# Attention and a two-layer network in one kernel: bank pairs declared as single tiles, one visit moved, some transfers queued later

## The chip, the cores and the metric

The kernel runs on one core of one Trainium2 chip. The metric is the device time of one execution in microseconds. The kernel before took 787.15 us, the median of three runs (785.26, 787.15 and 787.8).

## The reference

The input is q, k and v of shape 8 x 8 x 576 x 64 (batch, heads, sequence, head size) in float32. Each sequence is cut into chunks of 64 tokens, and a chunk attends only to itself. The result, with the heads side by side, is x, of 4608 tokens by 512, and goes through two matrix products with a leaky rectifier between them:

```python
scores = 1/sqrt(64) * q_c @ k_c.T            # per batch, head and chunk of 64 tokens
attn   = exp(scores - max(scores)); attn /= sum(attn) + 1e-9
x      = (attn @ v_c), heads side by side     # 4608 x 512
h      = x @ w_in                             # 512 -> 2048
g      = maximum(h, 0) + alpha * minimum(h, 0)
out    = g @ w_out                            # 2048 -> 512
```

## The kernel before

**Tiling.** The 4608 tokens are nine blocks of 512. The first three go through the network directly (lines L454 and L490 of the profile). The other six form three pairs, and a pair goes through both layers by a fast 2 x 2 block scheme with seven products in place of eight. Operands are split into a high and a low part, so each product is three passes. Attention works on blocks of 128 tokens; the attention for a pair is done beside the matmuls of the pair before it.

**A pair.** The first layer of a pair is eight steps (j = 0 to 7, `first_product`). A step holds seven sets of six matmuls on TensorE (`part`, line L764), in the order 5, 7, 1, 6, 3, 4, 2. They go into four PSUM banks: c takes sets 5 and 3, d takes 7 and 4, a takes 1 and 2, e takes 6. Between them ScalarE and VectorE read the banks: ScalarE copies c (L780) and a (L792), VectorE adds d and e to the copies (L781, L797, L798), then forms c+u and d+u (L807), and the rectifier is one ScalarE and one VectorE operation each (L439, L442). The names are: t is "gh", u is "g", h is "gl". After the eight steps the second layer follows (`second_product`, L895), seven products of 48 matmuls each, about 10.56 us each in the profile.

**Banks.** PSUM has eight banks here: two single tiles of the pool `ps_h` (taken anew at each use, two in turn), one tile of two banks `ps_a`, and two tiles of two banks, `ps_pa` and `ps_pb`. The last two pools open when the direct part's four accumulator banks (`ps_oa`, `ps_ob`) have been stored (L524). In a step, a and e are the halves of one `ps_pa` tile and change roles with the parity of j. In the first two pairs c and d are two `ps_h` tiles. In the last pair, where no attention is left, c and d are the halves of one `ps_pb` tile (`fronts`). The framework puts a wait where an instruction touches a tile that another engine still uses.

**Visits.** In the first two pairs, in steps 0, 2, 4 and 6, a joined visit (`joint_visit`) comes first on TensorE: the value products of up to two attention blocks (L420) and the score products of the next two (L289), into `ps_a` and `ps_pb`. The softmax of the new blocks (L301 to L308) and the transposition of 32 x 32 squares (L348, tile `t3`) follow inside the steps on VectorE and ScalarE. The last part of the transposition is done by eight DMAs of 32 KB, `pT<-t3` (L363, `move_blocks`); a value product needs them. There are two `pT` buffers. When both are taken, a block's moves wait in a list, and the next value products send them off at once. The q and k loads (L246, 256 KB each) of the next two blocks and the v loads (L250) go the same way, on SyncE's queue, in the order of issue. Weights stream on GpSimd's queue (L702), 512 KB at a time.

**Order.** A scheduler sets each engine's order. TensorE keeps the program's order; `high_priority` and `issue_after` steer the others.

Of the kernel before, what the change touches and what calls it, by code (L numbers as in the profile page):

```python
# [10 lines left out]
F32 = mybir.dt.float32  # L11
# [59 lines left out]
def tile_local_attention_prelu_ffn(  # L71
# [12 lines left out]
    nc = tc.nc  # L84
    P = 128
    NSUB, C = qT.shape[1], 64
# [8 lines left out]
    TB = 512  # L95
# [146 lines left out]
    def attn_load(s, parts="qkv"):  # L242
        if "q" in parts:
            q_sb, kb = (load.tile([P, H, C], F32, name=name, bufs=2) for name in ("q_sb", "k_sb"))
            for t, src in ((q_sb, qT), (kb, kT)):
                nc.sync.dma_start(out=t, in_=src[:, s].rearrange("p (h t) -> p h t", t=C))  # L246
            qkv[s] = [q_sb, kb, None]
        if "v" in parts:
            v_sb = load.tile([P, DM], F32, name="v_sb", bufs=2)
            loads.append(nc.sync.dma_start(out=v_sb, in_=v[:, s]))  # L250
            qkv[s][2] = v_sb
# [192 lines left out]
    def prelu(g, h, f):  # L444
        negative(g, h)
        rectify(g, h, f)
# [307 lines left out]
    def narrow():  # L754
        return [ps_h.tile([P, TB], F32, name="ps_h") for _ in range(2)]

    def product(ps, w, xs, first):

        passes = [(0, 0), (0, 1), (1, 0)]
        n = len(xs) * 3  # L760
        for m, (l, xl) in enumerate(passes):
            for k, xx in enumerate(xs):
                at = m * len(xs) + k
                pe(nc.tensor.matmul(  # L764
                    woven(ps), lhsT=w[:, l, k * P:(k + 1) * P], rhs=woven(xx[:, xl]),
                    start=first and at == 0, stop=at == n - 1, skip_group_check=not first,
                ))

    def first_product(ops, g, j, visited, fronts, ends, value):

        def part(ps, i, first):
            product(ps, weight("wi", i, j), [ops[i, k] for k in range(2)], first)

        c, d = fronts or narrow()
        a, e = ends[j % 2], ends[1 - j % 2]
        part(c, 5, True)
        part(d, 7, True)
        with tc.high_priority(offset=HIGH):
            t = gp.tile([P, TB], F32, name="gh")
            copied = nc.scalar.copy(t, c)  # L780
            nc.vector.tensor_tensor(t, d, t, op=ALU.add)  # L781
        if visited:
            with tc.high_priority(offset=HIGH), tc.issue_after(copied.ins):
                visit_softmax(*visited)
        part(a, 1, True)
        part(e, 6, True)
        if value is not None:
            with tc.high_priority(offset=HIGH):
                joint_values((value,))
        with tc.high_priority(offset=HIGH):  # L790
            u = gp.tile([P, TB], F32, name="g")
            copied = nc.scalar.copy(u, a)  # L792
        if visited:
            with tc.high_priority(offset=HIGH), tc.issue_after(copied.ins):
                visit_results(*visited)
        with tc.high_priority(offset=HIGH):
            nc.vector.tensor_tensor(u, e, u, op=ALU.add)  # L797
            nc.vector.tensor_tensor(t, t, u, op=ALU.add)  # L798
        for n, f in enumerate((j, JF + j)):
            g[f] = place(rooms[2 * j + n], [P, 2, TB], F32)  # L800
        with tc.high_priority(offset=HIGH):
            prelu(g[JF + j][:, 1], t, JF + j)
        for ps, i, f, col in ((c, 3, j, 1), (d, 4, JF + j, 0)):
            part(ps, i, False)
            with tc.high_priority(offset=HIGH):
                h = gp.tile([P, TB], F32, name="gl")
                nc.vector.tensor_tensor(h, ps, u, op=ALU.add)  # L807
                prelu(g[f][:, col], h, f)
        part(a, 2, False)
        with tc.high_priority(offset=HIGH):  # L810
            prelu(g[j][:, 0], a, j)

    CONVERT = (16, 17, 18, 20, 21, 23, 48, 49, 50, 51, 52, 53, 54, 55)
    AHEAD = 2
# [36 lines left out]
    def second_product(g, b, operands, conversion, end):  # L851
        y = [xp.tile([P, NK, TB], F32, name=name) for name in ("xh", "xl")]
        y11, y12, y21, y22 = y[0][:, :2], y[1][:, :2], y[0][:, 2:], y[1][:, 2:]

        def add(ys, ps):
            for m in range(2):
                nc.vector.tensor_tensor(ys[:, m], ps[m], ys[:, m], op=ALU.add)

        def finish(ys, ps):

            first = (b - PLAIN) * TB
            for m, queue in enumerate((nc.sync, nc.scalar)):
                nc.scalar.copy(ys[:, m], ps[m])
                queue.dma_start(out=outT[(2 + m) * P:(3 + m) * P, first:first + TB], in_=ys[:, m])

        def copy(ys, ps):
            for m in range(2):
                nc.scalar.copy(ys[:, m], ps[m])

        def done(ys, m, half, col):  # L870
            rows = slice((2 * half + m) * P, (2 * half + m + 1) * P)
            cols = slice((b - PLAIN + col) * TB, (b - PLAIN + col + 1) * TB)
            nc.sync.dma_start(out=outT[rows, cols], in_=ys[:, m])


        kept, third = narrow(), wide("ps_pb")
        for i in ORDERS["wo"]:
            if i == 2:
                ps = wide("ps_pa")
            else:  # L880
                ps = third if i in (5, 3) else kept
            for j in range(JF):
                at = JF * ORDERS["wo"].index(i) + j
                if at + AHEAD + EARLIER < 7 * JF:
                    difference(g, at + AHEAD + EARLIER)

                ahead = at + AHEAD + (at < 2)
                if at != 2 and ahead < 7 * JF:
                    with tc.high_priority(offset=2 * HIGH) if at < 2 else nullcontext():
                        operands.append(operand(g, ahead))  # L890
                hi, lo = operands.pop(0)
                w = weight("wo", i, j)
                for m in range(2):
                    for n, (l, xx) in enumerate(((0, hi), (0, lo), (1, hi))):
                        pe(nc.tensor.matmul(  # L895
                            woven(ps[m]), lhsT=w[:, l, m * P:(m + 1) * P], rhs=woven(xx),
                            start=i in (1, 5, 2) and j == 0 and n == 0, stop=j == JF - 1 and n == 2,
                            skip_group_check=i in (6, 7, 3, 4),
                        ))
                if conversion and at in CONVERT:  # L900
                    with tc.issue_after(behind[1][0].ins), tc.issue_after(behind[1][1].ins):
                        conversion.pop(0)()
            if i == 1:
                copy(y11, ps)
            elif i == 5:
                copy(y22, ps)
            elif i == 6:
                copy(y12, ps)
            elif i == 4 and end:
                finish(y21, ps)  # L910
            else:
                ys, half, col = {2: (y11, 0, 0), 7: (y22, 1, 1), 3: (y12, 0, 1), 4: (y21, 1, 0)}[i]
                (copy if i == 4 else add)(ys, ps)
                for m in range(2):
                    done(ys, m, half, col)
# [158 lines left out]
    def joint_values(olds):  # L1074
# [3 lines left out]
        outs = {}  # L1078
        for old in sorted((old for old in olds if old is not None), reverse=True):
            outs[old] = attn_values(old, 0, olds.index(old))  # L1080
        while moves and len(pdiag) < 2:
            move_blocks()
        for s in list(qkv):
            if qkv[s][2] is None and sum(e[2] is not None for e in qkv.values()) < 2:
                attn_load(s, "v")
        if len(olds) == 1:
            ended.append((olds[0], outs[olds[0]]))
        return outs

    VALUES = {0: (-2, -1), 2: (0, None), 4: (2, 1), 6: (4, 3)}  # L1090

    def joint_visit(base, j):
# [5 lines left out]
        for new in range(base + j + 2, base + j + 4):  # L1098
            if new < NSUB:
                attn_load(new, "q")  # L1100
        return [(old, outs.get(old), new, scores.get(new)) for old, new in zip(olds, news)]

    ended = []
    for pair in range(NPAIR):
# [5 lines left out]
        g = {}  # L1110
        joint = []
        for j in range(JF):
            if more and j in VALUES:
                with tc.high_priority(offset=HIGH):
                    joint = joint_visit(base, j)
            if j == 0:
                ends = wide("ps_pa")
                fronts = () if more else wide("ps_pb")
            visited = joint.pop(0) if joint else ()
            if j == JF - 1:  # L1120
                operands = [operand(g, at) for at in range(AHEAD + 1)]
            first_product(ops, g, j, visited, fronts, ends, base + 5 if more and j == JF - 1 else None)
        while ended:
            attn_x(*ended.pop(0))
        if more:
# [41 lines left out]
```

## Time and profile before

| | us |
|---|---|
| median of three runs | 787.15 |
| the profiled execution | 785.42 |
| its span, first to last instruction | 783.6 |
| TensorE busy (matmul) | 755.7 |
| VectorE busy | 651.8 |
| ScalarE busy | 447.5 |

The last pair's first layer runs from 618.63 to 706.00 us, the first pair's from about 300 to 387.5 us, and the second pair's from about 461.7 to 544.4 us. In the profile's rows PE is TensorE's matmuls, PEld its weight loads, DVE VectorE, ACT ScalarE, POOL GpSimd, SP SyncE; SPq is SyncE's queue of DMA issues. The granted clock of TensorE is at its full level in all 40 slices of the page.

### The profile page before, as it was taken

How to read it: one execution, taken by the hardware profiler on the slowest of the kernel's cores; microseconds unless marked ns; L12 is line 12 of the kernel's file. 1: busy time of each engine (PE TensorE's matmuls, PEld its weight loads, DVE VectorE, ACT ScalarE, POOL GpSimd, SP SyncE). 2: the span in 40 equal slices, each digit the busy share in tenths (PEclk: the TensorE clock that was granted, in tenths of full speed). 3: DMA queues.
4: the chain of work that ended last, by engine and by line, in shares of the span. 5: the costliest groups of instructions: out<-in, count | busy, mean ns of one | idle time of the engine just before them, and what ended most of it. 6: DMA issues, size and time to landing. Idle time of an engine off the chain costs nothing.

```text
span 783.6 us, 15264 instructions
## 1 busy us (share of the span) xinstructions
PE 755.7 (96%) x5515; PEld 632.3 (81%) x5516; DVE 651.8 (83%) x1142; ACT 447.5 (57%) x1181; POOL 183.3 (23%) x301
## 2 busy tenths in 40 slices
PE   5999999999999999998999999999999998889998
PEld 4888888888888887887888888888888776668886
DVE  6999999989899884877899888887998856669784
ACT  6965664676657654755656466665564533344543
POOL 1133332334352321111112111111121111111210
PEclk9999999999999999999999999999999999999999
DMA  9878785578697687877866787776667744455574
GB/s 358 329 252 318 283 290 168 195 229 245 224 261 238 224 286 238 265 221 239 296 219 197 253 279 257 245 241 206 200 204 245 260 166 161 161 188 185 191 247 156
DMA packets 69322, 184.52 MB, mean 235 GB/s; under 512 B 10992, under 2 KB 18176, under 8 KB 69120
## 3 DMA queue, kind: packets, MB, share of 16 engines
q0 software_dynamic: 34336, 119.56, 46.4%
q1 hardware_dynamic: 34480, 63.20, 24.0%
q8 instruction: 44, 0.72, 0.4%
q10 hardware_dynamic: 432, 0.79, 0.3%
q14 instruction: 30, 0.25, 0.1%
HBM read 135.27 MB, written 42.99 MB: 227 GB/s over the span
## 4 chain that ended last, share of the span: by engine, by line
PE 91%; DVE 3%; DMA 3%; ACT 1%; SPq 0%; issue 0%; ACTq 0%
PE ps_h L454 16%; PE ps_h L895 16%; PE ps_pa L764 11%; PE ps_h L764 9%; PE ps_oa L490 8%; PE ps_ob L490 8%; PE ps_pb L895 8%; PE ps_pb L764 4%; PE ps_pa L895 4%; PE ps_a L420 2%; PE ps_a L289 1%; DMA k_sb<-kT 1%; DMA wi<-qT 1%; DVE gh L798 1%; DVE g L797 1%; DVE gl L807 1%
## 5 line engine op out<-in xcount | busy, mean ns | idle before, releaser
L454 PE MATMUL ps_h<-xh,wi 128*128 128x512 f32 x384 | 100.1, 384 | 0.0
L454 PEld LDWEIGHTS ps_h<-xh,wi 128*128 128x128 f32 x384 | 71.0, 187 | 12.7
L721 ACT CAST gh<-wo 128x512 fp32r<-128x512 f32 x66 | 41.0, 621 | 48.2 <-PE ps_h L895 20.1
L490 PE MATMUL ps_oa<-wo,gh 128*128 128x512 f32 x192 | 58.1, 383 | 0.0
L490 PE MATMUL ps_ob<-wo,gh 128*128 128x512 f32 x192 | 57.6, 380 | 0.0
L722 DVE TENSOR_TENSOR gl<-wo,gh 128x512 fp32r<-128x512 f32 x63 | 43.3, 687 | 12.3 <-ACT gh L721 12.0
L764 PE MATMUL ps_pa<-wi,raw 128*128 128x512 f32 x216 | 52.2, 382 | 0.2 <-DVE wo L442 0.2
L304 ACT ACTIVATE pr<-ps_a,mx 128x64 f32<-128x64 f32 x168 | 50.5, 325 | 0.7
L454 PE MATMUL ps_h<-xl,wi 128*128 128x512 f32 x192 | 50.1, 381 | 0.0
L702 POOL DMA_DIRECT2D raw<-wi_a x42 | 22.4, 533 | 112.3 <-PE ps_h L764 41.5
L764 PEld LDWEIGHTS ps_pa<-wi,raw 128*128 128x128 f32 x216 | 40.2, 187 | 8.1 <-DVE wo L442 1.1
L764 PE MATMUL ps_h<-wi,raw 128*128 128x512 f32 x192 | 46.1, 384 | 0.3 <-DMA raw<-wi_a 0.3
L702 POOL DMA_DIRECT2D raw<-wo_a x42 | 22.3, 531 | 89.0 <-PE ps_h L895 38.0
L468 ACT CAST gh<-g 128x512 fp32r<-128x512 f32 x48 | 30.1, 629 | 21.9 <-DVE g L442 11.5
L454 PEld LDWEIGHTS ps_h<-xl,wi 128*128 128x128 f32 x192 | 35.8, 187 | 6.8 <-ACT xl L405 0.4
L764 PEld LDWEIGHTS ps_h<-wi,raw 128*128 128x128 f32 x192 | 35.5, 187 | 7.0 <-DVE t L348 0.6
L490 PEld LDWEIGHTS ps_ob<-wo,gh 128*128 128x128 f32 x192 | 35.9, 187 | 6.4
L490 PEld LDWEIGHTS ps_oa<-wo,gh 128*128 128x128 f32 x192 | 35.6, 187 | 6.4
L721 ACT CAST ta<-wo 128x512 fp32r<-128x512 f32 x42 | 26.2, 623 | 24.2 <-PE ps_h L895 13.8
L439 ACT ACTIVATE g<-ps_h 128x512 f32<-128x512 f32 x48 | 29.4, 613 | 17.6 <-PE ps_h L454 17.6
L721 ACT CAST more<-wo 128x512 fp32r<-128x512 f32 x42 | 25.9, 618 | 22.7 <-DVE wo L829 10.7
L722 DVE TENSOR_TENSOR more<-wo,more 128x512 fp32r<-128x512 f32 x42 | 28.8, 686 | 10.1 <-ACT more L721 10.1
(332 smaller groups left out, 2099.5 us busy)
## 6 DMA issues: line engine op xcount, KB each, us to landing
raw<-wi_a POOLq DMA_DIRECT2D x42, 512.0 KB, 4.5
raw<-wo_a POOLq DMA_DIRECT2D x42, 512.0 KB, 4.0
wi<-wi_a POOLq DMA_DIRECT2D x21, 512.0 KB, 4.1
wo<-wi_a POOLq DMA_DIRECT2D x21, 512.0 KB, 4.7
wi<-wo_a POOLq DMA_DIRECT2D x21, 512.0 KB, 3.7
wo<-wo_a POOLq DMA_DIRECT2D x21, 512.0 KB, 3.7
v_sb<-v SPq DMA_DIRECT2D x28, 256.0 KB, 4.6
q_sb<-qT SPq DMA_DIRECT2D x28, 256.0 KB, 6.5
```

Of the source, the lines that this page charges most:

```text
L289: pe(nc.tensor.matmul(att[pair][c * C:(c + 1) * C, par, (at + hp) * C:(at + hp + 1) * C], lhsT=q_sb[rows, 2 * hp + c], rhs=kb[rows, 2 * hp ...
L304: last = nc.scalar.activation(pr[:, g], sc3[:, g // NP, g % NP], AF.Exp, bias=mx[:, g], scale=SCALE, accum_out=sm[:, g])
L420: pe(nc.tensor.matmul(att[pair][par * C:(par + 1) * C, c, (at + hp) * C:(at + hp + 1) * C], lhsT=v_sb[rows, h * C:(h + 1) * C], rhs=p[rows ...
L439: nc.scalar.activation(g, h, AF.Relu, scale=-1.0)
L454: pe(nc.tensor.matmul(woven(hps), lhsT=wi[f][:, l, k * P:(k + 1) * P], rhs=woven(xx[:, k]), start=(i == 0 and k == 0), stop=(i == 2 and k ...
L468: nc.scalar.copy(gh, g)
L490: pe(nc.tensor.matmul(woven(o), lhsT=a[:, ts], rhs=woven(wo[f][:, l]), start=(f == first and i == 0), stop=(f == last and i == 2),))
L702: streamed[0] = nc.gpsimd.dma_start(out=f32(t), in_=units[side][n])
L721: hi = nc.scalar.copy(t_hi, t)
L722: return hi, nc.vector.tensor_tensor(t_lo, t, f32(t_hi), op=ALU.subtract)
L764: pe(nc.tensor.matmul(woven(ps), lhsT=w[:, l, k * P:(k + 1) * P], rhs=woven(xx[:, xl]), start=first and at == 0, stop=at == n - 1, skip_gr ...
L895: pe(nc.tensor.matmul(woven(ps[m]), lhsT=w[:, l, m * P:(m + 1) * P], rhs=woven(xx), start=i in (1, 5, 2) and j == 0 and n == 0, stop=j == ...
```

## The change

There are three parts.

1. A new helper `single()` gives two tiles of one bank each. It takes the place of `wide("ps_pa")` for a and e and for the second layer's product 2. `fronts` is gone, so that c and d come from `narrow()` (two `ps_h` tiles) in all three pairs.
2. In the first pair's step 0 the joined visit is a callable that `first_product` calls behind sets 5 and 7.
3. `joint_values` no longer sends off the waiting block moves and the v loads. A new function `after_values` does that. `joint_visit` calls it behind the q and k loads, and the block moves in it are put behind the last of these loads (`stages["scored"]`).

```diff
+                stages["scored"] = nc.sync.dma_start(out=t, in_=src[:, s]...)
...
+    def single():
+        return [ps_p.tile([P, TB], F32, name=f"ps_p{n}") for n in range(2)]
...
-        c, d = fronts or narrow()
+        c, d = narrow()
         a, e = ends[j % 2], ends[1 - j % 2]
         part(c, 5, True)
         part(d, 7, True)
+        rest = ()
+        if callable(visited):
+            with tc.high_priority(offset=HIGH):
+                visited, *rest = visited()
...
-                ps = wide("ps_pa")
+                ps = single()
...
-        while moves and len(pdiag) < 2:
-            move_blocks()
+        return outs
+
+    def after_values():
         for s in list(qkv):
             if qkv[s][2] is None and sum(e[2] is not None for e in qkv.values()) < 2:
                 attn_load(s, "v")
+        with tc.issue_after(stages["scored"].ins):
+            while moves and len(pdiag) < 2:
+                move_blocks()
...
         for new in range(base + j + 2, base + j + 4):
             if new < NSUB:
                 attn_load(new, "q")
+        after_values()
...
-                ends = wide("ps_pa")
-                fronts = () if more else wide("ps_pb")
+                ends = single()
```

On TensorE, in the last pair's first step, the rows before are these (the first matmul of each of the seven sets 5, 7, 1, 6, 3, 4, 2, then of set 5 of the next step; the number behind a tile's name is its buffer):

```order
L764 MATMUL ps_pb_7478<-wi6_7376,raw_7398 128x4x32x4
...
L764 MATMUL ps_pb_7478<-wi4_7046,raw_7398 128x4x32x4
...
L764 MATMUL ps_pa_7477<-wi0_6978,raw_7427 128x4x32x4
...
L764 MATMUL ps_pa_7477<-wi8_7407,raw_7427 128x4x32x4
...
L764 MATMUL ps_pb_7478<-wi10_7435,wi15_7451 128x4x32x4
...
L764 MATMUL ps_pb_7478<-wi12_7460,wi15_7451 128x4x32x4
...
L764 MATMUL ps_pa_7477<-wi2_7007,wo15_7479 128x4x32x4
...
L764 MATMUL ps_pb_7478<-wi6_7376,wo15_7479 128x4x32x4
```

The same place on TensorE in the changed kernel:

```order
L768 MATMUL ps_h_7483<-wi6_7380,raw_7402 128x4x32x4
...
L768 MATMUL ps_h_7484<-wi4_7049,raw_7402 128x4x32x4
...
L768 MATMUL ps_p0_7481<-wi0_6981,raw_7431 128x4x32x4
...
L768 MATMUL ps_p1_7482<-wi8_7411,raw_7431 128x4x32x4
...
L768 MATMUL ps_h_7483<-wi10_7439,wi15_7455 128x4x32x4
...
L768 MATMUL ps_h_7484<-wi12_7464,wi15_7455 128x4x32x4
...
L768 MATMUL ps_p0_7481<-wi2_7010,wo15_7485 128x4x32x4
...
L768 MATMUL ps_h_7556<-wi6_7380,wo15_7485 128x4x32x4
```

The order of the sets is the same; the four banks of a step are four tiles instead of two, and set 5 of the next step takes a new tile.

On TensorE at the start of the first pair, before (value products L420, score products L289, then the first set of step 0):

```order
L490 MATMUL ps_ob_2854<-wo15_1643,gl_3849 128x4x32x4
L420 MATMUL ps_pb_3928<-pT_3658,v_sb_3637 64x64 x16
L420 MATMUL ps_a_3927<-pT_3514,v_sb_3493 64x64 x16
L289 MATMUL ps_a_3927<-k_sb_3490,q_sb_3489 64x64 x16
L289 MATMUL ps_pb_3928<-k_sb_3634,q_sb_3633 64x64 x16
L764 MATMUL ps_h_4006<-wi6_3764,raw_3877 128x4x32x4
...
L764 MATMUL ps_h_4007<-wi4_3755,raw_3877 128x4x32x4
...
L764 MATMUL ps_pa_4005<-wi0_3391,raw_3879 128x4x32x4
```

The same place in the changed kernel:

```order
L491 MATMUL ps_ob_2854<-wo15_1643,gh_3847 128x4x32x4 x2
...
L768 MATMUL ps_h_3929<-wi6_3764,raw_3877 128x4x32x4
...
L768 MATMUL ps_h_3930<-wi4_3755,raw_3877 128x4x32x4
...
L421 MATMUL ps_pb_3944<-pT_3658,v_sb_3637 64x64 x16
L421 MATMUL ps_a_3943<-pT_3514,v_sb_3493 64x64 x16
L290 MATMUL ps_a_3943<-k_sb_3490,q_sb_3489 64x64 x16
L290 MATMUL ps_pb_3944<-k_sb_3634,q_sb_3633 64x64 x16
L768 MATMUL ps_p0_3927<-wi0_3391,raw_3879 128x4x32x4
```

The twelve matmuls of sets 5 and 7 now stand between the direct part's last matmul and the visit; set 1 follows the visit.

On SyncE in the first pair, before, from the visit of step 4 on (eight moves of the waiting block 3, two v loads, two pairs of q and k loads, the moves of blocks 4 and 5, and the next v load):

```order
L363 DMA pT_4488<-t3_4416 32x256 x8
L250 DMA v_sb_4497<-v 128x512
L250 DMA v_sb_4499<-v 128x512
L246 DMA q_sb_4533<-qT 128x512
L246 DMA k_sb_4534<-kT 128x512
L246 DMA q_sb_4537<-qT 128x512
L246 DMA k_sb_4538<-kT 128x512
L363 DMA pT_4595<-t3_4593 32x256 x8
L363 DMA pT_4766<-t3_4694 32x256 x8
L250 DMA v_sb_4775<-v 128x512
```

The same place in the changed kernel:

```order
L251 DMA v_sb_4529<-v 128x512
L251 DMA v_sb_4531<-v 128x512
L247 DMA q_sb_4521<-qT 128x512
L247 DMA k_sb_4522<-kT 128x512
L247 DMA q_sb_4525<-qT 128x512
L247 DMA k_sb_4526<-kT 128x512
L364 DMA pT_4533<-t3_4417 32x256 x8
L364 DMA pT_4596<-t3_4594 32x256 x8
L251 DMA v_sb_4807<-v 128x512
```

The moves of the block that was waiting (`t3_4416`, now `t3_4417`: block 3 of this pair's visits) went ahead of the six loads of step 4 and now follow them; the moves of block 5 (`t3_4694`) go behind the six loads of step 6 in the same way.

## Rows read from the trace of the kernel before

**Rows 1.** The page, part 1: busy us, share of the span, instructions.

```profile
PE 755.7 (96%) x5515; PEld 632.3 (81%) x5516; DVE 651.8 (83%) x1142; ACT 447.5 (57%) x1181; POOL 183.3 (23%) x301
```

**Rows 2.** Waits of PE, 300 to 784 us: total us, times, longest.

```profile
PE ps_pb L764 <- DVE gl L807: 11.2, 8, 1.4
PE ps_a L420 <- DMA pT<-t: 2.2, 1, 2.2
PE ps_pb L420 <- ACT wo L524: 1.2, 1, 1.2
```

**Rows 3.** Waits of PE's weight loads, the same stretch.

```profile
PEld ps_pa L764 <- DVE wo L442: 1.9, 7, 0.6
```

**Rows 4.** The chain of waits, last pair, step 0: start us, us, what.

```profile
618.63 2.64 PE ps_pb L764 x12
...
623.95 0.59 ACT g L792
...
625.98 0.61 DVE gl L807
626.64 1.59 PE ps_pb L764 x6
...
629.55 2.64 PE ps_pb L764 x12
...
706.00 10.56 PE ps_h L895 x48
```

**Rows 5.** The chain of waits, second pair, step 1.

```profile
473.24 2.64 PE ps_h L764 x12
475.88 2.75 PE ps_pa L764 x12
...
482.63 0.62 PE ps_a L420 x32
```

**Rows 6.** Busy us by engine in last pair's first layer, granted clock, DMA, GB/s.

```profile
618.63:706.00 87.37, 76.16 (x337) 62.22 (x337) 54.06 (x80) 33.77 (x57) 14.86 (x28) 1.00 0.53 177
```

**Rows 7.** Timeline, ScalarE at the last pair's start.

```profile
618.01 0.59 ACT L868 COPY xh<-ps_h 128x512 f32<-128x512 f32 x1 [2.90 <-PE ps_h L895]
```

**Rows 8.** The chain of waits, first pair, step 0.

```profile
298.93 1.08 ACT wo L524 x2
...
300.06 0.84 PE ps_pb L420 x29
...
302.36 2.86 PE ps_h L764 x12
...
311.82 0.22 PE ps_h L764
```

**Rows 9.** Timeline, the same step: copy of c, first exponential, VectorE's sums L807.

```profile
303.99 0.59 ACT L780 COPY gh<-ps_h 128x512 f32<-128x512 f32 x1 [3.98 <-PE ps_h L764]
...
304.71 0.31 ACT L304 ACTIVATE pr<-ps_a,mx 128x64 f32<-128x64 f32 x1
...
310.32 1.28 DVE L807 TENSOR_TENSOR gl<-ps_h,g 128x512 f32<-128x512 f32 x2
```

**Rows 10.** The chain of waits, first pair, steps 4 to 7.

```profile
341.55 0.62 PE ps_a L420 x32
...
351.74 9.54 DMA k_sb<-kT
361.29 4.09 DMA pT<-t
365.42 0.63 PE ps_a L420 x27
...
382.70 0.62 PE ps_a L420 x32
```

**Rows 11.** Timeline, SyncE: the v loads of step 4 in the first pair.

```profile
348.27 1.08 SPq L250 DMA_DIRECT2D v_sb<-v  x2
```

**Rows 12.** The moves `pT<-t`, 300 to 470 us: issue to landing.

```profile
DMA to landing us min/median/max: 1.8/4.4/8.0
```

More of the change, by code (lines that the diff above doesn't have):

```diff
@@ L1 @@
+import functools
 import re
@@ L245, in attn_load @@
             for t, src in ((q_sb, qT), (kb, kT)):
-                nc.sync.dma_start(out=t, in_=src[:, s].rearrange("p (h t) -> p h t", t=C))
+                stages["scored"] = nc.sync.dma_start(out=t, in_=src[:, s].rearrange("p (h t) -> p h t", t=C))
             qkv[s] = [q_sb, kb, None]
@@ L767, in product, with first_product @@
                 ))
-    def first_product(ops, g, j, visited, fronts, ends, value):
+    def first_product(ops, g, j, visited, ends, value):
         def part(ps, i, first):
             product(ps, weight("wi", i, j), [ops[i, k] for k in range(2)], first)
-        c, d = fronts or narrow()
+        c, d = narrow()
         a, e = ends[j % 2], ends[1 - j % 2]
@@ L788, in first_product @@
             with tc.high_priority(offset=HIGH):
-                joint_values((value,))
+                ended.append((value, joint_values((value,))[value]))
+                after_values()
         with tc.high_priority(offset=HIGH):
@@ L811, in first_product @@
             prelu(g[j][:, 0], a, j)
+        return list(rest)
     CONVERT = (16, 17, 18, 20, 21, 23, 48, 49, 50, 51, 52, 53, 54, 55)
@@ L1085, in joint_values @@
                 attn_load(s, "v")
-        if len(olds) == 1:
-            ended.append((olds[0], outs[olds[0]]))
-        return outs
+        with tc.issue_after(stages["scored"].ins):
+            while moves and len(pdiag) < 2:
+                move_blocks()
     VALUES = {0: (-2, -1), 2: (0, None), 4: (2, 1), 6: (4, 3)}
@@ L1100, in joint_visit @@
                 attn_load(new, "q")
+        after_values()
         return [(old, outs.get(old), new, scores.get(new)) for old, new in zip(olds, news)]
@@ L1112, in tile_local_attention_prelu_ffn @@
         for j in range(JF):
-            if more and j in VALUES:
+            visit_here = more and j in VALUES
+            if visit_here and pair + j > 0:
                 with tc.high_priority(offset=HIGH):
@@ L1116, in tile_local_attention_prelu_ffn @@
             if j == 0:
-                ends = wide("ps_pa")
-                fronts = () if more else wide("ps_pb")
-            visited = joint.pop(0) if joint else ()
+                ends = single()
+            if visit_here and pair + j == 0:
+                visited = functools.partial(joint_visit, base, j)
+            else:
+                visited = joint.pop(0) if joint else ()
             if j == JF - 1:
                 operands = [operand(g, at) for at in range(AHEAD + 1)]
-            first_product(ops, g, j, visited, fronts, ends, base + 5 if more and j == JF - 1 else None)
+            rest = first_product(ops, g, j, visited, ends, base + 5 if more and j == JF - 1 else None)
+            joint = rest or joint
         while ended:
```

## The prediction

> **What bounds the kernel now.** I read the page's first part, then the waits of TensorE, then the chain of waits from the first pair to the end, and the timeline at its gaps. TensorE's matmuls are busy 755.7 us of the span [rows 1], so this kernel is bound by TensorE, and only a gap in front of a matmul, or a delay that makes a new one, moves the time. Behind 300 us nearly all gaps are three waits: 11.2 us in eight waits for a VectorE sum of the last pair, 2.2 us once for the block moves, 1.2 us once for a ScalarE store [rows 2]. The weight loads add small waits for a rectifier [rows 3]. The change has a part for each of these four. No matmul is added or taken away, and before the first pair the order of the engines is the same.
>
> **The last pair's banks.** A step of the last pair runs from 618.63 to 629.55, that is 10.92 us, and all eight take 706.00 - 618.63 = 87.37 us [rows 4]. Twelve matmuls without a wait take 2.64 us [rows 4], so 42 take 3.5 x 2.64 = 9.24, and 1.68 per step is lost. The chain shows where. Sets 1 and 6 end at 623.9, ScalarE's copy of a starts only then, VectorE's sums follow, and set 4 starts at 626.64, right behind the sum c+u (L807), which reads c and not set 4's bank d. Set 4 waits since c and d are one tile; the copy of a waits for e's matmuls for the same reason. With four tiles set 4 needs only the earlier sum t = d + t, and the copy of a can start 1.32 us sooner, when set 1 has ended. What is late next: set 5 of the next step needs c read by c+u. That sum is done 2.7 us behind set 6 (623.9 to 626.6 [rows 4]), and sets 3, 4 and 2 take 3.96, so nothing. The nearest measured case is the second pair, where c and d are already two tiles: its step 1 takes 482.63 - 473.24 = 9.39 [rows 5], with more work on VectorE. So the gain lies between 87.37 - 8 x 9.39 = 12.2 and 87.37 - 8 x 9.24 = 13.5; I take 13.0, since the 0.11 in that row's sets 1 and 6 goes too (next part). One new wait: set 5 of the first step now takes a `ps_h` tile that the second pair's last product held, and ScalarE's copy of it runs from 618.01 to 618.60 [rows 7], just ahead of the set's start in the chain at 618.63 [rows 4]. I take 0.2 lost for the handover, at most the 0.6 of a copy. VectorE is busy 54.06 us there [rows 6]; in 74 us that is 73%, so it doesn't become the bound. The granted clock is 1.00 there already, so nothing comes from the clock. Term: **-12.8** (-11.6 to -13.5).
>
> The rule that different banks need no order between them is in the Trainium skill, "PSUM — Partial Sum Buffer", section "PSUM bank collisions raise a hardware error": guard by bank and 32-partition quadrant, not more widely. The trace shows the wait between two banks but not whether the chip or the program asks for it; by the rule the term is the full one, and if the wait were the chip's it would be 0, which is the rival "the wait stays" below.
>
> **The same split in the first two pairs.** In step 1 of the second pair sets 1 and 6 take 2.75 where 2.64 is the work [rows 5]: set 1 goes to the bank free since e was read, but waits for the rectifier that reads the old a. The weight loads waited so seven times, 1.9 us in all [rows 3]. With two tiles only set 6 waits, 1.32 later, and nobody then. Seven times 0.11 is 0.8; I take **-0.7** (0 to -1.9).
>
> **The first pair's first visit.** TensorE stops from 298.9 to 300.06 until ScalarE's stores (298.93, 1.08 long) have freed the banks that the visit takes [rows 8]. Sets 5 and 7 go into `ps_h`, which is free, and fill 2.64 us. The visit, 300.06 to 302.36, then runs at about 301.5 to 303.8, and sets 1, 6, 3, 4 and 2 with the restart of 0.2 end at 310.6, where before the next step's set 5 begins at 311.82 [rows 8]: -1.2 if nothing follows late. But the softmax now starts 1.5 later against that end. Before, the first sum c+u ended at 310.96, the first of the two in its row [rows 9], 8.6 us behind the visit. Kept at 8.6 behind 303.8 it would end at 312.4 and hold the next step's set 5 by 1.8: then the part loses 0.6. But of the 8.6, ScalarE's queue held the first exponential until 304.71 [rows 9], as it stood behind the copy of c (303.99 and 0.59 long [rows 9]); the scores were there at 302.36 and the maximum needs some 0.9 more, so 1.4 of it goes, and the wait shrinks to 0.2 to 0.4. I take **-0.9** (+0.6 to -1.3).
>
> **The queued block moves.** SyncE's queue issues in order, and the chain shows that a transfer is held until the one eight places ahead has landed: the eighth move behind the last k load is issued when that load lands (351.74 + 9.54 = 361.28), and lands at 365.38 [rows 10]. The value products of step 6 waited for it from 363.2 on. Now the loads of step 4 go first. The v loads need only the value products that start at 341.55, so they move from 348.27 [rows 11] to about 342.2, and the last k load, which landed 13.0 behind the first v load, lands at 355.2. But block 3's eight moves stand between it and block 4's: block 3's last goes at 355.2 and lands 4.4 later (the median [rows 12]), and block 4's last goes with that landing, 359.6, and lands at 364.0, against 363.2 where TensorE is ready. So 0.8 of the 2.2 stays. With two landings of 1.8 all 2.2 goes; with two of 8.0 the stall is 8.0. I take the median, whose nearest case is the 4.09 of the chain [rows 10]: -1.4.
>
> In step 6 the same edit costs where there is no wait now. Block 5's moves now stand behind six loads. First v load at about 366.0, last k load 13.0 later at 379.0, block 5's last move lands at 383.4, and its value product stands at 382.70 [rows 10]: +0.7, from 0 to 4.3 with a landing of 8.0. The transposition on VectorE that needs the buffer back is late by as much in steps 5 and 7; the visit and the second layer's start cover that. Together **-0.7** (-2.2 to +10.1).
>
> [...]
>
> **Sum.** -12.8 - 0.7 - 0.9 - 0.7 = -15.1. The profiled execution took 785.42, its span 783.6 and 1.8 around it, so the same execution would take 770.3. It was one of the faster ones; from the median of 787.15 the forecast is **772.0**.
>
> **Rivals.**
> *Late block moves.* The two waits in steps 6 and 7 grow. For it: both estimates miss by under 1 us, and landings reach 8.0 [rows 12]. Against: the median is 4.4, and part of the queue now starts 6 us sooner. At 6.2 a landing, midway, block 4 lands at 367.6 and block 5 at 385.2: stalls of 4.4 and 2.5, so the part is +4.7 in place of -0.7, and the time 777.4.
> *Another wait takes the place in the last pair.* The rectifier of a (L442) or the sum c+u ends last in each step. For it: 0.6 was its longest hold on a weight load [rows 3]. Against: the second pair's 9.39. Eight times 0.6 is 4.8, so 776.8.
> *The wait stays.* Set 4 still waits for the later sum, since a count of VectorE's work has to pass it. For it: every sum comes from one engine in order. Against: the sum that set 4 needs is the first of the step. Then the other parts alone: 787.15 - 2.3 = 784.9.
> *Slower.* One mechanism: the deferred moves at step 6 and 7 of the first pair and at one visit of the second miss their value products by the longest landing each. 8.0 + 4.3 in the first pair are +10.1 net, and 8.0 in the second make 18.1; with -14.4 from the rest that is 790.9. It decides from 14.4 us of new stalls on. Against: only one visit of the second pair has both loads and a waiting block, and it shows no such wait now.
>
> **How the numbers follow.** Forecast 0.78 (own range 769 to 775, from the bounds of the first three terms), late moves 0.10, another wait 0.07, the wait stays 0.03, slower 0.02. The runs before spread over 2.5 us, 0.3% of the time, which is also what a measurement can tell from no change. The range goes from 768.5 (the gains at their upper ends, 13.5 + 0.8 + 1.3 + 2.2 = 17.8, and 0.8 for the spread) to 777.5 and takes in the late moves and the other wait; what lies above has 0.06 with the tail of those two. Faster by over 0.3% (below 784.8) holds the forecast, the two middle rivals and half of "the wait stays": 0.96; within 0.3% the other half, 0.02; slower 0.02.
>
> **What would show it.** Right: in the last pair a step of about 9.27 us, no wait of set 4 for L807, ScalarE's copy of a beginning while set 6 runs; sets 1 and 6 at 2.64 everywhere; at 299 us twelve `ps_h` matmuls without a gap and set 5 of step 1 within 0.4 of ready; block 4's value product waiting under 1 us and block 5's about as long. Wrong: a step of the last pair over 9.5, a wait in front of step 1's set 5 over 1.5, or a value product in steps 6 or 7 that waits over 2 us for the moves.

## The result, and the profile after

The changed kernel takes 767.63 us (median of 6 runs, 767.19 to 769.24); the kernel before, in runs beside it and those shown above, 786.43 (783.22 to 787.80). The ratio is 0.977, with a 95% interval of 0.9749 to 0.9791. That is faster, as forecast, but 4.4 us below the forecast of 772.0 and 0.9 below the lower end of its range. The profiled execution took 767.25 with a span of 765.5, 18.2 under the one of before where the sum said 15.1: that is 3.1 of the 4.4. The other 1.3 is the allowance from profiled execution to median, 1.73 in the forecast and 0.38 here.

The page's first part answers to [rows 1]: busy us, share of the span, instructions.

```profile
PE 753.4 (98%) x5516; PEld 633.6 (83%) x5516; DVE 648.3 (85%) x1142; ACT 444.4 (58%) x1181; POOL 182.2 (24%) x301
```

TensorE's work is what it was (755.7 before). Of the 18.1 us, 15.8 are idle time of its matmuls; the other 2.3 are busy time of the same matmuls, and why they count less of it is not shown. The list of waits behind 295 us, which answers to [rows 2] and [rows 3], has no row of PE any more. Two rows of the weight loads' are these (us in total, times, longest):

```profile
PEld ps_a L421 <- issue: 2.1, 6, 0.3
...
PEld ps_h L768 <- DVE gl L816: 0.8, 2, 0.5
```

TensorE's waits for L807 and for `pT` are gone, and so is the one for the rectifier (L442 before); two weight loads still wait for the sum (L816 is L807 of before). To see where the time came from, I cut both traces at the same matmuls: the last matmul of the direct part, then the first matmul of a visit, of block 5's value product, of a layer. Us:

| stretch | before | after | difference | forecast |
|---|---|---|---|---|
| first pair, last matmul of the direct part to the visit of step 2 | 22.60 | 21.55 | -1.05 | -0.9 and split |
| to the visit of step 4 | 20.37 | 20.27 | -0.10 | split |
| to the visit of step 6 | 21.43 | 20.72 | -0.71 | split |
| to block 5's value product in step 7 | 19.72 | 16.76 | -2.96 | moves -0.7, and split |
| to the second layer | 4.72 | 4.69 | -0.03 | 0 |
| second pair, first layer | 82.58 | 82.25 | -0.33 | split |
| last pair, first layer | 87.37 | 74.06 | -13.31 | -12.8 |

The split of the first two pairs was forecast at -0.7 over all its stretches. What is not in the table (both second layers, the end, the time ahead) changes by +0.4 in sum.

The chain of waits in the last pair answers to [rows 4]: start us, us, what. A step is 623.18 - 613.64 = 9.54 the first time and (687.86 - 623.18) / 7 = 9.24 from then on, which is 42 matmuls and nothing else. The first set's 2.94 holds 0.3 for the handover of its tile.

```profile
613.64 2.94 PE ps_h L768 x12
616.58 2.64 PE ps_p L768 x12
619.22 2.64 PE ps_h L768 x12
621.86 1.32 PE ps_p L768 x6
623.18 2.64 PE ps_h L768 x12
...
687.86 10.56 PE ps_h L905 x48
```

Lines of the timeline of the same step (start us, us, engine, line, what, idle before and its releaser) show what the chain can't, the work beside it:

```profile
617.94 0.58 ACT L801 COPY g<-ps_p 128x512 f32<-128x512 f32 x1 [1.48 <-PE ps_p L768]
...
620.66 0.68 DVE L816 TENSOR_TENSOR gl<-ps_h,g 128x512 f32<-128x512 f32 x1
```

ScalarE's copy of a starts at 617.94, while set 6 still runs (to 619.22 by the chain), and sets 3 and 4 follow it at once. The sum c+u (L816) starts at 620.66, when set 4, which it used to hold up, already runs (the second half of the twelve matmuls from 619.22 on).

In the first pair the chain answers to [rows 8] and [rows 10]: sets 5 and 7 stand ahead of the visit, no gap follows them, and the visits of steps 4 and 6 and block 5's value product come without a wait.

```profile
299.07 2.65 PE ps_h L768 x12
301.72 0.62 PE ps_pb L421 x32
...
310.00 0.61 DVE gl L816
...
310.65 3.04 PE ps_h L768 x12
...
340.57 0.62 PE ps_a L421 x32
...
361.29 0.62 PE ps_a L421 x32
...
378.05 0.62 PE ps_a L421 x32
```

Step 1's set 5 starts at 310.65, right behind the sum L816 (310.00 + 0.61), and the chain goes back from there over the softmax, not over TensorE. The set was held: its twelve matmuls take 3.04 where 2.64 is the work, and the weight loads' wait for L816 above is up to 0.5. That is the wait of 0.2 to 0.4 that was forecast.

### The profile page after: what moved, and what is told of

It is laid out like the page before. It is cut to its first block, busy times and chain, and to the rows that moved or that the text cites. A ratio compares the mean times of both kernels' runs of the same rounds, so it can differ in the third digit from the quotient of the medians.

```text
span 765.5 us, 15287 instructions
## 1 busy us (share of the span) xinstructions
PE 753.4 (98%) x5516; PEld 633.6 (83%) x5516; DVE 648.3 (85%) x1142; ACT 444.4 (58%) x1181; POOL 182.2 (24%) x301
## 4 chain that ended last, share of the span: by engine, by line
PE 97%; ACT 1%; DMA 1%; DVE 0%; issue 0%; ACTq 0%
PE ps_h L455 17%; PE ps_h L905 17%; PE ps_h L768 17%; PE ps_p L768 12%; PE ps_oa L491 8%; PE ps_ob L491 8%; PE ps_pb L905 8%; PE ps_p L905 4%; PE ps_a L421 2%; PE ps_a L290 1%; DMA wo<-qT 1%; PE ps_pb L421 0%; PE ps_pb L290 0%; ACT wo L331 0%; ACT pr L305 0%; ACT wi L331 0%
## 5 line engine op out<-in xcount | busy, mean ns | idle before, releaser
L768 PE MATMUL ps_h<-wi,raw 128*128 128x512 f32 x288 | 68.8, 382 | 0.0
L768 PEld LDWEIGHTS ps_h<-wi,raw 128*128 128x128 f32 x288 | 53.5, 187 | 10.1 <-ACT xh L878 0.4
L768 PE MATMUL ps_p<-wi,raw 128*128 128x512 f32 x216 | 52.0, 381 | 0.0
L768 PEld LDWEIGHTS ps_p<-wi,raw 128*128 128x128 f32 x216 | 40.3, 187 | 7.1
L440 ACT ACTIVATE wo<-gh 128x512 f32<-128x512 f32 x24 | 15.2, 632 | 48.7 <-DVE gh L807 48.7
L469 ACT CAST gh<-g 128x512 fp32r<-128x512 f32 x48 | 30.2, 629 | 21.6 <-DVE g L443 11.2
L722 ACT CAST more<-wo 128x512 fp32r<-128x512 f32 x42 | 25.9, 618 | 20.9 <-DVE wo L839 10.7
```

The source lines that it names most:

```text
L440: nc.scalar.activation(g, h, AF.Relu, scale=-1.0)
L469: nc.scalar.copy(gh, g)
L722: hi = nc.scalar.copy(t_hi, t)
L768: pe(nc.tensor.matmul(woven(ps), lhsT=w[:, l, k * P:(k + 1) * P], rhs=woven(xx[:, xl]), start=first and at == 0, stop=at == n - 1, skip_gr ...
```

## The experiments

Each takes one part of the change alone or leaves one out, or disturbs the one part whose price was doubtful. "Before" beside them is 785.16 us for the first four, 784.29 for the next four, 785.42 for the last two.

**Only c and d as single tiles in the last pair.** Against before:

```diff
-        c, d = fronts or narrow()
+        c, d = narrow()
...
```

> The kernel before with c and d as two single tiles in the last pair too; a and e stay one tile, no visit and no transfer is moved. Theory (the gain of the last pair is set 4's false wait on the other bank of its pair): set 4 no longer waits for the sum c+u, a step of the last pair takes 9.35 to 9.4 us as in the second pair, so the last pair gains 12 to 12.5 us and the whole is about 774 us against 786.4. Rival (the split of a and e carries most of it, since ScalarE's copy of a starts the chain late): a step stays above 10 us and the gain is under 7 us.

Measured 770.96 us, ratio 0.9819 (0.9790 to 0.9849). The last pair's first layer takes 74.04 us, all that the whole change gains there. The chain of waits there:

```profile
617.83 2.92 PE ps_h L765 x12
620.75 2.64 PE ps_pa L765 x12
```

No gap between them, and sets 1 and 6 are at 2.64 though a and e are still one tile here (`ps_pa`). The step is 74.04 / 8 = 9.25, not the 9.35 to 9.4 expected: the 0.11 that [rows 5] has in sets 1 and 6 is not there in a pair without a softmax on VectorE.

**Only a and e as single tiles.** Against before:

```diff
-                ends = wide("ps_pa")
+                ends = single()
```

and the same for the second layer's product 2.

> The kernel before with a and e as two single tiles in all pairs; c and d stay halves of one tile in the last pair, no visit and no transfer is moved. Theory: the copy of a leaves the chain behind set 6, so set 4's wait of 1.4 us shrinks by the copy's 0.6 to about 0.8 in each of eight steps (5 us), and some 0.7 us of small waits in the first two pairs go: about 780.5 us. Rival (a and e carry most of the last pair's gain): about 774 us.

Measured 780.01 us, ratio 0.9939 (0.9919 to 0.9959). The last pair takes 83.00. Waits of PE:

```profile
PE ps_pb L768 <- DVE gl L815: 6.8, 8, 0.9
...
PE ps_a L421 <- DMA pT<-t: 2.3, 1, 2.3
```

Set 4 still waits for the sum that reads c (L815 here), only 0.55 less each time, since the copy of a starts earlier and so does the sum. The chain shows on what it hangs, the sums behind sets 1 and 6 (the copy of a is out of it):

```profile
623.20 2.65 PE ps_p L768 x12
...
625.95 0.70 DVE g L805
...
627.36 0.61 DVE gl L815
...
628.02 1.59 PE ps_pb L768 x6
```

So the wait is the shared tile c, d. The two edits are not two halves: the one on c and d takes 13.3, the one on a and e 4.4 by itself, and in the last pair nothing on top of the first (74.04 against 74.06 in the whole change).

**Only the queued moves.** Against before, the v loads and `move_blocks` go into `after_values`, as in the change, nothing else.

```diff
+        with tc.issue_after(stages["scored"].ins):
+            while moves and len(pdiag) < 2:
+                move_blocks()
...
```

> The kernel before with only the queue order changed: the v loads and the waiting block moves behind the q and k loads. Theory (the order alone removes the wait of step 6 in the first pair, and with it late weights, as the loads now go out while the weight stream pauses for the visit): no wait for the moves in steps 6 and 7, steps 4 to 7 of the first pair 3 to 3.7 us shorter, about 783 us. Rival (the shorter steps come from the other two parts, which start them sooner): within 0.7 us of before, and the wait of about 2 us stays.

Measured 783.13 us, ratio 0.9981 (0.9966 to 0.9997). Waits of PE:

```profile
PE ps_pb L765 <- DVE gl L813: 11.2, 8, 1.4
PE ps_pb L421 <- ACT wo L525: 1.2, 1, 1.2
```

The wait for `pT` is gone, not shortened to 0.8. The stretch to block 5's product is 17.52 (19.72 before), and that from step 4 to 6 is 20.82 (21.43): -2.8 together, in one execution of each. By the medians it is -2.0 (785.16 to 783.13).

**Only the first visit.** Against before:

```diff
+            if visit_here and pair + j == 0:
+                visited = functools.partial(joint_visit, base, j)
...
```

> The kernel before with only the first joined visit moved behind sets 5 and 7. Theory: the wait of 1.16 us for ScalarE's stores goes, and set 5 of step 1 waits 0.2 to 0.5 us more for the sum c+u; with a and e still one tile the copy of a comes 1.3 us later than in the changed kernel, but it is behind the exponentials anyway, so the gain is about 0.9 us, 785.5. Rival: the softmax's delay gives all of it back, within 0.3 us of before.

Measured 783.18 us, ratio 0.9971 (0.9953 to 0.9988). The stretch from step 0 to step 2 is 22.03 against 22.60: -0.57. Waits of PE:

```profile
PE ps_a L421 <- DMA pT<-t: 1.1, 1, 1.1
```

By the medians it is -2.0 (785.16 to 783.18), more than the stretch has; steps 4 to 7 are shorter too in this execution, with the old queue order. The wait of 1.2 for the store is gone. Half of it comes back, in set 2 of step 0, whose weight load waits 0.5 for the sum that reads e, and in step 1, where the chain goes over the later softmax:

```profile
310.99 1.20 DVE gl L812 x2
312.19 2.65 DVE wo L443 x4
...
314.89 2.93 PE ps_pa L765 x12
```

Not set 5 waits, as the forecast feared, but sets 1 and 6: they go to the shared tile of a and e, which the rectifier (L443) still reads. With the split they don't. The wait for `pT`, too, is 1.1 here, 1.4 and 2.3 in the first two runs and 1.4 in the next, in kernels with the same order of SyncE's queue: its size is not fixed, and I had read one execution of it.

**The change without its moves.** Against after, `move_blocks` and the v loads go back to where before has them.

> The changed kernel with the old queue order: waiting block moves and v loads ahead of the q and k loads. Theory (the order is worth 2.8 to 4 us with the other parts in place too): steps 4 and 5 of the first pair take 21.1 to 21.4 us in place of 20.7, step 6 waits 1.2 to 3.6 us for the moves, in all about 771 us. Rival (the other parts start the steps so much sooner, or space them so, that the old order also fits): within 0.5 us of the changed kernel.

Measured 770.54 us, ratio 0.9816 (0.9782 to 0.9849); the change itself, run beside it (below), 0.9788. Waits of PE:

```profile
PE ps_a L421 <- DMA pT<-t: 1.4, 1, 1.4
...
PE ps_h L768 <- DMA raw<-wi_a: 0.8, 1, 0.8
...
PE ps_p L768 <- DMA wi<-wi_a: 0.3, 1, 0.3
```

Beside the wait for the moves there are two that I had not priced: weights that come late, right behind the loads. (The kernel before has one such row, of 0.3 us.) By stretch the moves are worth 1.04 from step 4 to 6 and 2.30 behind it, by the medians 2.3 in all.

From the visit of step 4 to block 5's product, the five kernels with the old queue order (before, those with c and d, a and e or the visit alone, and this one) take 39.5 to 42.3 us. The four executions with the change's order (the change twice, the moves alone, and the change without single tiles below) take 37.5 to 38.3.

**The change without single tiles for a and e** (and for the second layer's product 2).

```diff
-                ends = single()
+                ends = wide("ps_pa")
```

> The changed kernel with a and e as one tile of two banks; the other three edits stay (c and d as single tiles, the visit, the queue order). Theory (with c and d apart, a and e matter only where VectorE is loaded with the softmax): the last pair stays at 74.0 to 74.1 us; the first pair's step 0 and 1 lose about 0.5 us and its steps 6 and 7 about 0.7, the second pair 0.3 to 0.6, in all 769 us. Rival (the split of a and e is needed in the last pair): the last pair takes 75 us or more, about 769 as well, so the last pair's length tells it.

Measured 769.06 us, ratio 0.9792 (0.9772 to 0.9812). By stretch it is 0.47 longer to step 2, 0.53 in steps 6 and 7 and 0.86 in the second pair, and the same in the last (74.06). The weight loads wait again for the rectifier:

```profile
PEld ps_pa L765 <- DVE wo L443: 2.2, 6, 0.7
```

**The change once more**, no edit, as the measure of these four and of its own spread.

> The changed kernel itself, on the same chip as the three others, to compare their stretches with it: 766 to 769 us; TensorE waits for nothing in steps 4 to 7 of the first pair, though block 4's last move lands within 0.5 us of its use. If that margin is luck, a wait of up to 1 us shows here.

Measured 768.22 us, ratio 0.9788 (0.9760 to 0.9816), with no wait for the moves or the weights in the first pair. Its profiled execution took 771.14; the last section has more on it.

**Loads late again.** The question behind this and the next two: the forecast took 13.0 us for the six loads, measured they took 10.7. Is that the order in the queue, or the moment? Here the loads of steps 4 and 6 stay ahead of the moves, as in the change, but start only behind ScalarE's copy of a (two VectorE operations on one column, of no use to the output, hold them), and the v loads go behind q and k.

```diff
+                    for q_old, k_old in old:
+                        nc.vector.scalar_tensor_tensor(table, in0=q_old[:, 0, :1], scalar=u[:, :1], in1=k_old[:, 0, :1], op0=ALU.mult, op1=ALU.add)
+                    loads_now()
...
```

> The changed kernel, but in steps 4 and 6 of the first pair the q and k loads are held until ScalarE has copied a (about 6 us behind the visit, where the old order issued them), by two tiny VectorE operations on the old q and k tiles; v loads and block moves follow the loads. Their results go nowhere. Theory (a load's time depends on when it goes out: during the visit the weight stream pauses, and later it shares the DMA engines with a full stream): the last k load takes 8 us or more from issue to landing, and the six loads over 11.8 us from the first issue, against 6.6 and 10.7 in the changed kernel; TensorE waits some 6 to 8 us for the moves in each of steps 6 and 7, about 780 us. Rival (the loads were slow before because the moves stood ahead of them in the queue; the moment does not matter): last k load at most 6.8 us, six loads at most 10.8 us, waits of 3 to 5 us each, about 775 us.

Measured 783.98 us, ratio 0.9995 (0.9979 to 1.0011): this alone gives the whole gain back. The six loads of step 4 start 8.1 us later than in the change and take 10.6 in all (349.35 to 359.95), in the order q, k, q, k, v, v; those of step 6 take 11.1. Waits of PE, and SyncE's timeline:

```profile
PE ps_a L421 <- DMA pT<-t: 11.0, 3, 5.4
```

```profile
349.35 0.34 SPq L247 DMA_DIRECT2D q_sb<-qT  x1
...
352.35 13.49 SPq L364 DMA_DIRECT2D pT<-t  x16
```

The waits of 11.0 us lie between the two answers (12 to 16 for the theory, 6 to 10 for the rival), and the loads' 10.6 and 11.1 are under the theory's 11.8. This run alone does not decide.

**Moves ahead of the loads.** Against after, eight transfers of 32 KB, as large as the moves, into a buffer that nobody reads, ahead of the loads of steps 4 and 6. The v loads go behind q and k there.

```diff
+                ahead = nc.sync.dma_start(out=extra[n], in_=held[rows, n % 2].rearrange("p h t -> p (h t)"))
...
```

> The changed kernel with eight extra transfers of 32 KB (the value block just used, written to a scratch place in DRAM that nobody reads) ahead of the six loads of steps 4 and 6 in the first pair, where the old order had block 3's and 5's moves; then q, k, q, k, v, v, then the waiting moves. Theory (the old order's six loads took 11.2 to 13.1 us from first issue to last landing because eight transfers stood just ahead of them): over 11 us in both steps. Rival (what stands ahead does not matter, 8 to 10.7 us without it and 13.0 before was one of several lengths): under 10.8 us. Either way the loads start some 4 us later than in the changed kernel, so TensorE waits some 3 to 6 us for the moves in step 6, and the whole is 774 to 782 us.

Measured 768.62 us, ratio 0.9777 (0.9719 to 0.9835). Waits of PE:

```profile
PE ps_a L421 <- DMA pT<-t: 1.2, 1, 1.2
```

Neither the waits of 3 to 6 us nor the time of 774 and more came: the loads of step 4 started at 342.10, only 0.9 us later than in the change, and those of step 6 at 365.29. SyncE's timeline has the extra transfers ahead of them:

```profile
335.15 4.90 SPq L1115 DMA_DIRECT2D extra<-pT  x8
...
360.08 3.92 SPq L1115 DMA_DIRECT2D extra<-pT  x8
```

The six loads took 12.0 at step 4 and 9.3 at step 6. Against the expectation that is one for each answer; the run to compare with is the next one, which has the same six loads in the same order without the extra transfers.

**Loads first, late order.** Against after, the v loads go behind q and k, at the moment of the change. From the run that held the loads it differs in the moment, and by the two small VectorE operations.

```diff
-        after_values()
+        with tc.issue_after(stages["scored"].ins):
+            after_values()
```

> The changed kernel with the v loads behind the q and k loads at each visit of step 4 and 6 (the order of the late-loads run, at the visit's own time). Theory (moment does not matter): six loads take 9.3 to 10.8 us from the first issue, as in the changed kernel and in the late-loads run, and no wait for the moves over 1 us; about 768 us. Rival (the pause of the weight stream speeds them): under 9 us here against 10.6 in the late-loads run.

Measured 768.93 us, ratio 0.9781 (0.9725 to 0.9837).

The six loads, from 341.98 on, take 8.1 us at step 4 and 8.1 at step 6, against 10.6 and 11.1 in the same order with the loads held (7.4 us later at step 4). So the moment counts, by 2.5 to 3.0 us here. The run with transfers ahead, in this order too and from 342.10 on at step 4, took 3.9 and 1.2 longer: what stands ahead counts as well, though one execution of each shows it, and kernels with one and the same order differ by up to 1.9 at step 4 (below). The stretch from step 4 to 6 is 21.69, 0.97 longer than in the change, and TensorE waits 0.7 there for a rectifier; why, I did not settle.

## Why the prediction came out 4.4 us too high

Of the 3.1 us that the profiled executions differ from the sum, the moves are 2.1, the split 1.1 (of which 0.4 in the first stretch) and the last pair with its handover 0.3; the first visit alone gives 0.3 back.

**The last pair: right.** Forecast -12.8, measured -13.3, inside the bounds. The mechanism is the one named: c and d in one tile made set 4 wait for a sum that reads c. That the run with c and d alone gets it all answers the rivals "the wait stays" and "another wait takes the place". The last half microsecond was the bound from below, 9.24 a step, which is reached from the second step on; the handover, put at 0.2, is 0.3 in the first set (2.94 in place of 2.64).

The Trainium skill, "PSUM — Partial Sum Buffer", section "PSUM bank collisions raise a hardware error", says to guard PSUM by bank and quadrant, and that pairs of engines on different banks ran clean. The full gain of 13.3 us agrees with it: the wait was the program's.

**The first visit: right, though part of it hangs on the split.** The visit starts behind sets 5 and 7 without a gap. Alone it gives -0.57, with the split -1.05, where -0.9 and one of the split's seven times 0.11 were forecast. What I took for the risk came: set 5 of step 1 is held by the sum, its twelve matmuls taking 0.4 more.

**The split in the rest of the first two pairs: right in its mechanism, too small.** With the moves (-0.61 and -2.20) taken out by their own run, the table leaves 0.10 + 0.10 + 0.76 + 0.33 = 1.3 for it, where six times 0.11 were forecast. The run without it says 1.97 for all its stretches, and 0.8 by the medians. I had taken the one hold of 0.11 that stood in a chain and multiplied; the list had the total, 1.9 [rows 3], which is nearer. That 1.9 was the term's stated bound, yet the low end of the range, "the gains at their upper ends", adds 0.8 in its place: with 1.9 the gains are 13.5 + 1.9 + 1.3 + 2.2 = 18.9 and the end is 787.15 - 18.9 - 0.8 = 767.45.

**The queued moves: the step that failed.** It is "the last k load, which landed 13.0 behind the first v load, lands at 355.2", and with it "so 0.8 of the 2.2 stays". Forecast -0.7 in all; measured -2.8 by the stretches of its own run, beyond the bound of -2.2, and -2.0 by the medians. The v loads did move, from 348.27 [rows 11] to 341.25. SyncE's timeline of the change:

```profile
341.25 2.28 SPq L251 DMA_DIRECT2D v_sb<-v  x2
...
345.33 0.43 SPq L247 DMA_DIRECT2D k_sb<-kT  x1
345.86 11.83 SPq L364 DMA_DIRECT2D pT<-t  x16
```

The last k load landed at 351.91, 10.66 behind the first v load and not 13.0. Block 4's last move then went at 357.10 and landed at 361.07; by the timeline TensorE starts on the block at 361.22, 0.15 behind the landing and without a wait. The rest of that step came out as worked: the two landings in the queue behind the loads took 5.19 and 3.97 for 4.4 each, and the first load went 0.7 behind the value products of its visit, as forecast; all work there comes some 1.0 us sooner. So the failure is one duration, 2.3 us too long, which turned a rest of 0.8 into a margin of 0.15. In the five kernels with the old order the six loads of step 4 take 11.2 to 13.1 us, in the four executions with the change's order 9.3 to 10.7: the forecast took one execution's 13.0, near the top of the old order's, for the new one.

Why 13.0 did not carry over: windows of both traces, with the busy us of each engine, the granted clock, the DMA engines' mean busy share and GB/s. Before:

```profile
341.00:350.00 9.00, 9.00 (x160) 7.62 (x159) 6.30 (x12) 5.46 (x23) 1.59 (x3) 1.00 0.60 187
350.00:361.00 11.00, 10.74 (x49) 8.68 (x48) 9.30 (x17) 6.83 (x26) 2.12 (x4) 1.00 0.95 326
```

After:

```profile
341.00:350.00 9.00, 9.00 (x145) 7.83 (x135) 6.04 (x12) 4.33 (x21) 1.45 (x3) 1.00 0.92 304
350.00:361.00 11.00, 11.00 (x52) 9.26 (x50) 9.32 (x17) 7.50 (x26) 2.12 (x4) 1.00 0.86 261
```

Before, the DMA engines were 0.60 busy just behind the visit, since SyncE sent only small moves there; then the six loads met the weight transfers of the next steps, at a share of 0.95. After, the loads fill the slack, and the stretch behind them has room. The two orders of this kernel keep to it: the five kernels with the old queue order have 0.54 to 0.60 and then 0.95 to 1.01, the four executions with the change's 0.85 to 0.92 and then 0.79 to 0.86. The loads themselves are part of these shares, and a share alone does not give a duration: the held loads took 10.6 with 1.01 in the second stretch. The stretch from step 4 to 6 is also the part of the gain that I had not priced: in three of the five kernels with the old order TensorE waited here for weights (1.1 us in the run without the moves, 0.4 in the one with c and d alone), and the stretch is 0.6 shorter by the moves' own run. I had bounded the gain by the wait for the moves; a transfer of another queue was late too, and the list of before has it (total us, times, longest):

```profile
PE ps_h L764 <- DMA raw<-wi_a: 0.3, 1, 0.3
```

The run with late loads bears out the cause of the wait (the loads' start decides when the moves land: 8.1 us later made 11.0 us of waits), and loads first shows that the moment is worth 2.5 to 3.0 us on six loads. The run with transfers ahead, set against loads first, puts 3.9 and 1.2 us on what stands ahead, as far as one execution of each tells. The change does away with both, the late moment and the eight moves ahead of the loads. What stays open is how the 2.3 us divide between the two.

**Block 5's moves.** Forecast +0.7, with the same 13.0; measured nothing. The loads at step 6 start at 361.97 and their q and k land 6.7 to 7.3 us behind their issue, the last at 371.9, where 379.0 was forecast. Block 5's product comes at 378.05 without a wait.

**The rivals of late moves and of slower.** They did not come, and they were near: with the loads 8.1 us later TensorE waits 11.0 us for the moves, and the whole change is worth nothing.

The Trainium skill, "DMA: Bandwidth & Descriptors", section "Queues, rings and completion order", says that descriptors are consumed in ring order on each DMA engine, and also that completion need not follow the order of issue. The run with late loads agrees with the first: its first move, issued at 352.35 behind the six loads, landed at 360.79, behind the last load at 359.95. What the rule cannot tell, and where I went wrong, is how long the loads ahead take.

## What to carry to other kernels

When TensorE waits for an engine that reads a bank which the matmul doesn't write, look first whether two banks are one tile; here that was 13.3 us of 18.1, and the lower bound (matmuls alone) was reached. Don't carry a transfer's duration to another moment or another place in the queue: the same six loads took from 8.1 to 13.1 us at step 4, by when they went out and what stood ahead, so forecast with the whole range. Price a family of small waits by the total in the list of waits, not by one of them times their count. And add up a range from the bounds that the terms have.

## What was not expected of the hardware

After a stand of TensorE the granted clock can fall. With the loads late, TensorE waits 5.4 us for the moves at step 6, at a granted clock of 1.00 until then; the windows behind it (columns as above):

```profile
360.00:370.00 10.00, 4.46 (x109) 3.76 (x111) 5.22 (x8) 2.89 (x5) 0.53 (x1) 0.72 0.57 186
370.00:380.00 10.00, 10.00 (x79) 8.54 (x73) 6.14 (x13) 4.68 (x22) 1.48 (x3) 0.94 0.32 110
```

From 367.4 to 369.4 the granted clock is 0.50, the lower level of 1.2 GHz; the chain has 1.02 us there for the 27 value products that take 0.63 in the kernel before [rows 10]. So a wait can cost more than its length: the three stretches are 5.65 + 7.14 + 2.80 = 15.6 us longer than in the change, for 11.0 us of waits.

It does not always fall: the kernel before stays at 1.00 behind its wait of 2.2 us, and the run with a and e alone, behind one of 2.3, has this:

```profile
367.20:370.60 3.40, 3.40 (x89) 3.09 (x82) 1.41 (x3) 0.00 (x0) 0.00 (x0) 0.50 0.13 31
```

The change's second profile shows the fall without any wait. Its chain:

```profile
499.69 0.11 PE ps_pb L290 x5
499.80 1.82 issue
501.63 0.67 PE ps_pb L290 x26
502.30 4.51 PE ps_h L768 x12
```

In the midst of equal score products TensorE stood for 1.82 us, with nothing in the profile to wait for, and the twelve matmuls behind it took 4.51, in place of 2.85 at this place in the first execution. The windows around it:

```profile
489.00:497.00 8.00, 8.00 (x38) 6.81 (x37) 6.55 (x13) 5.11 (x23) 1.58 (x3) 1.00 0.92 311
497.00:505.00 8.00, 6.18 (x140) 4.98 (x139) 4.36 (x7) 1.58 (x3) 0.53 (x1) 0.84 0.65 216
```

The stand and the matmuls behind it at the lower level make the 4.0 us by which this execution's second pair is longer (86.21 against 82.25). What stopped the engine is not shown. One thing differs there: a 16 KB transfer of the instruction queue runs from 499.00 to 500.23, over the start of the stand, which the first execution had begun at 496.36, ahead of the visit.
